# Attention's keys and values: one transfer over 128 partitions in place of two over 64

## The chip, the cores and the metric

The kernel runs on one core of a Trainium2 chip. The metric is device time in microseconds (us). The engines of the core are TensorE (PE in the profile: matrix products), VectorE (DVE), ScalarE (ACT), GpSimd (POOL) and SyncE (SP), which here issues every transfer. Sixteen DMA engines move the data between DRAM and the on-chip memory of 128 partitions.

## The reference

One pre-norm transformer block over 2,048 rows of 640 columns in float32: attention in a local, dilated window, then a gated feed-forward network.

```python
def _A_ref(x, wqkv, wo):
    H = 32; Dh = D // H                  # D = 640, Dh = 20
    W, dil = 8, 2
    qkv = (x @ wqkv).reshape(B, S, 3, H, Dh).transpose(2, 0, 3, 1, 4)
    q, k, v = qkv[0], qkv[1], qkv[2]
    idx = pos[:, None] - off[None, :]    # off = arange(W) * dil
    mask = idx >= 0
    ...
    logits = jnp.einsum("bhsd,bhswd->bhsw", q, kg) * Dh ** -0.5
    attn = softmax(where(mask, logits, -1e9))
    o = jnp.einsum("bhsw,bhswd->bhsd", attn, vg)
    return o.transpose(0, 2, 1, 3).reshape(B, S, D) @ wo

h = x + _A_ref(layernorm(x), wqkv, wo)
h2 = h + (silu(layernorm(h) @ w_gate) * (layernorm(h) @ w_up)) @ w_down   # F = 1728
```

Each row looks at itself and at the seven rows 2, 4, ..., 14 before it. Rows of even and of odd number never meet in attention; they are called the two parities below.

## The kernel before, in words

The 2,048 rows are cut into four blocks (b = 0 to 3) of 512. In a block, partitions 0 to 63 hold the 256 rows of one parity and partitions 64 to 127 those of the other, four consecutive rows of a parity (j) in each partition. The 32 heads are cut into four groups (g) of eight heads, 160 columns each. So attention has 16 steps (b, g).

`qkv` (line 532) computes queries, keys and values of one (b, g) on TensorE (line 552, in three passes that make up for the reduced precision of the products). ScalarE moves the sums into a staging tile `st` (line 557), which has room for two (b, g). From there `put` (line 563) stores the keys into the DRAM tensor `ksc` and the values into `vsc`, in two transfers each, one for each parity; the queries go to `qsc` in one (line 572). `ksc` and `vsc` have the shape [group, parity, 1,031 rows, 160 columns]; the first seven rows of each plane are zeros, the halo before the first row, which `zero_halo` (line 275) writes once in one transfer over 8 partitions for each tensor.

`att_load` (line 582) loads a step: the queries in two transfers (line 588), then keys and values (line 593). A partition needs its own four rows and the seven before, 11 rows of 160 columns or 7,040 bytes in one run, and neighbouring partitions' runs overlap: start every 640 elements, length 1,760. Again there is one transfer for each parity. Keys and values share three slots of 1,760 columns in turn, so the keys of one step take the place of the values of the step before the last, and its values that of the keys of the step before.

VectorE then does all of attention but the exponential: the products of queries and keys and their sums (`att_qk`, lines 603 and 610, twice per step), the maximum and the sum of the softmax (lines 617 to 634), the products with the values (line 638) and the sums over the window (line 646, lines 652 to 676). SyncE stores the result in 8 small transfers per step (line 680) into `osc`, from which the output projection `wo` (line 749, products at line 801) takes it. The feed-forward network of blocks 0, 1 and 2 (products at lines 871, 882, 966, 988) is computed between the attention steps; weights come from `ffn_in` (line 847), and their low-order parts go to DRAM once (`lsc`, line 860) and come back from there (lines 853, 1052, 1068).

What runs when is set by a planner. Every piece of work is put on record with an engine, a cost, what it reads and writes and a priority (`P.add`). `Plan.order` (line 74) plays these through with its own costs (for transfers: the bytes, the number of pieces and a fixed landing time) and so gets a start time for each piece; the table `SHIFT` moves the start times of some pieces, named by their number; the pieces are then written out in the order of these times, which fixes the order on each engine and on SyncE's queue. SyncE issues in that order, and waits at a transfer whose data or room are not there yet.

Of the kernel before, what the change touches and what calls it, by code (L numbers as in the profile page):

```python
# [20 lines left out]
NB, NJ, NG, NC = 4, 4, 4, 5  # L21
GC = D // NG
SEQ = S // 2 + W - 1
# [12 lines left out]
PR = {'x': 0.5, 'yst': 8, 'yld': 2, 'wqd': 4, 'wqh': 0.5, 'wql': 4, 'qev': 1, 'kvs': 0.4, 'atl': 1.2, 'exp': 0.5, 'ost': 3, 'wod': 2, 'woh': 8, 'wol': 1.2, 'old': 1.5, 'fld': 4, 'lst': 6, 'wev': 1.5, 'fh': 2.2, 'fl': 8, 'ln1': 8, 't1': 1, 'wo0': 1.2, 'wo': 2.2, 'ln1t': 1.2, 'xb': 0.4, 'tr': 10, 't1t': 2.2, 'ln1d': 0.5, 'hst': 10, 'hld': 10, 'ht': 1, 'hc': 2, 'jd': 3, 'jp': 8, 'js': 4, 'jl': 0.4, 'ja': 0.5, 'jfld': 1.2, 'jfh': 4, 'jfl': 1, 'jhi': 4, 'jmu': 0.4, 'jlo': 0.9, 'jcm': 0.5, 'w3': 1, 'w3e': 8, 'w3o': 0.4, 'w3x': 8, 'w3l': 2.2, 'jy': 6}  # L36

SHIFT = {
# [8 lines left out]
}  # L47


# [107 lines left out]
def nb(chunks, size):  # L157
    return (chunks / 16 * 0.042 + chunks * size / 435e3) * RATE


def act(n):
    return 0.155 + 0.00087 * n


def program(tc, x_in, wqkv_in, wo_in, ffn_in, ffl_in, const_in, out):
    nc = tc.nc
    V, A, T, Q, G = nc.vector, nc.scalar, nc.tensor, nc.sync, nc.gpsimd
    P = Plan()
# [4 lines left out]
    with tc.tile_pool(name="sb", bufs=1) as sb, tc.tile_pool(  # L173
        name="ps", bufs=1, space=PSUM
    ) as psp, tc.tile_pool(name="dr", bufs=1, space=DRAM) as dr, tc.manual_schedule():
        fa = sb.tile([128, FA_N], F32, name="fa")
# [30 lines left out]
        def stage_t():  # L207
            if "st" not in late:
                late["st"] = sb.tile([128, 3840], F32, name="st", tag="ab")
            return late["st"]  # L210
# [41 lines left out]
        def f(o, n):  # L252
            return fa[:, o : o + n]

        def rf(o, n):
            return ("fa", o, o + n)

        def r_(o, n):
            return ra[:, o : o + n]

        def rr(o, n):
            return ("ra", o, o + n)

        def pb(i):
            return (f"b{i}", 0, 1)
# [14 lines left out]
        for nm, t in (("K", ksc), ("V", vsc)):  # L280
            P.add(
                "SP", 0.07, lambda t=t: zero_halo(t), r=[rf(PROD, 1120)],
                w=[(f"{nm}{g}{a}", 0, 7) for g in range(NG) for a in range(2)], prio=6, nbytes=36e3,
# [180 lines left out]
        def wq(g, half, k):  # L464
            return 4800 * g + 2400 * half + 480 * k

        def xt(b):
            t = sha_t if b % 2 == 0 else (lambda: shb)
            nm = "sha" if b % 2 == 0 else "shb"
            return t, nm  # L470
# [61 lines left out]
        def qkv(b, g):  # L532
            t, nm = xt(b)
            so = 1920 * (qn[0] // NJ % 2)
            passes = ((0, 0), (1, 0), (0, 1))
            whole = [(p, c) for p in range(3) for c in range(NC)]
            if b == g == 0:
                whole = [x for c in range(NC + 1) for x in ([(0, c)] if c < NC else []) + ([(1, c - 1), (2, c - 1)] if c else [])]
            first_mm, last_mm = whole[0], whole[-1]
            for j in range(NJ):  # L540
                bk = qn[0] % 5
                qn[0] += 1
                moved = (b, g, j) == (NB - 1, NG - 1, NJ - 1)
                if moved:
                    P.add("ACT", act(640), lambda j=j: A.copy(r_(XH, 640), t()[:, 640 * j : 640 * j + 640].bitcast(F32)), r=[(nm, 640 * j, 640 * j + 640)], w=[rr(XH, 640)], prio=3)

                def mm(ps, j=j, bk=bk, moved=moved):
                    for p, c in ps:
                        a, w = passes[p]
                        o = 2560 * a + 640 * j + 128 * c  # L550
                        l = r_(XH + 128 * c, 128) if moved and a == 0 else t()[:, o : o + 128]
                        T.matmul(banks[bk][:, 0:480], l, r_(wq(g, w, c), 480), start=(p, c) == first_mm, stop=(p, c) == last_mm)  # L552
                for ps in [[x] for x in whole] if b == g == 0 else [whole]:
                    P.add("PE", 0.218 * len(ps), lambda ps=ps, mm=mm: mm(ps),
                          r=[x for p, c in ps for x in (rr(XH, 640) if moved and passes[p][0] == 0 else (nm, 2560 * passes[p][0] + 640 * j + 128 * c, 2560 * passes[p][0] + 640 * j + 128 * c + 128), rr(wq(g, passes[p][1], c), 480))],
                          w=[pb(bk)], prio=10)
                P.add("ACT", act(480) + 0.06, lambda bk=bk, j=j: A.activation(  # L557
                    stage_t()[:, so : so + 1920].rearrange("p (t j c) -> p t j c", t=3, j=NJ)[:, :, j, :],
                    banks[bk][:, 0:480].rearrange("p (t c) -> p t c", t=3), AF.Identity, scale=f(RS1 + 4 * b + j, 1)),
                    r=[pb(bk), rf(RS1 + 4 * b + j, 1)], w=[("ab", so + 480 * j, so + 480 * j + 480)], prio=PR["qev"])  # L560

            def put(par, dst, o):
                Q.dma_start(
                    dst[g, par, 7 + 256 * b : 7 + 256 * b + 256, :].rearrange("(r j) c -> r (j c)", j=NJ),
                    stage_t()[64 * par : 64 * par + 64, o : o + 640],
                )
            for nmd, dst, o in (("K", ksc, so + 640), ("V", vsc, so + 1280)):
                for par in range(2):
                    P.add("SP", 0.65, lambda par=par, dst=dst, o=o: put(par, dst, o), r=[("ab", so, so + 1920)],
                          w=[(f"{nmd}{g}{par}", 1000 + 256 * b, 1256 + 256 * b)], prio=PR["kvs"], nbytes=nb(64, 2560))  # L570
                if nmd == "K":
                    P.add("SP", 0.65, lambda: Q.dma_start(qsc[b, g].rearrange("p j c -> p (j c)"), stage_t()[:, so : so + 640]),
                          r=[("ab", so, so + 1920)], w=[(f"Q{b}{g}", 0, 4)], prio=PR["kvs"], nbytes=nb(128, 2560))
# [8 lines left out]
        def att_load(b, g):  # L582
            n = an[0]
            an[0] += 1
            ko, vo = KV + 1760 * (2 * n % 3), KV + 1760 * ((2 * n + 1) % 3)
            qo, lo, mo = QT, LG + 256 * (n % 2), MX + 64 * (n % 2)
            for h in range(2):
                P.add("SP", 0.45, lambda h=h: Q.dma_start(f(qo + 320 * h, 320), qsc[b, g, :, 2 * h : 2 * h + 2, :].rearrange("p j c -> p (j c)")), r=[(f"Q{b}{g}", 0, 4)], w=[rf(qo + 320 * h, 320)], prio=PR["atl"], nbytes=nb(128, 1280))
            for nmd, dst, o in (("K", ksc, ko), ("V", vsc, vo)):
                for par in range(2):  # L590
                    def ld(dst=dst, o=o, par=par):
                        a = dst[g, par, 256 * b, :]
                        Q.dma_start(fa[64 * par : 64 * par + 64, o : o + 1760],
                                    bass.AP(tensor=a.tensor, offset=a.offset, ap=[[640, 64], [1, 1760]]))
                    lo_r = 0 if b == 0 else 1000 + 256 * (b - 1)
                    P.add("SP", 0.45, ld, r=[(f"{nmd}{g}{par}", lo_r, 1000 + 256 * (b + 1))], w=[(f"fakv{par}", o, o + 1760)], prio=PR["atl"], nbytes=nb(64, 7040))
            return b, g, n, ko, vo, qo, lo, mo

        two_keys = []
# [586 lines left out]
        def ln2_columns(b, prio):  # L1186
# [8 lines left out]
            for u in range(5):  # L1195
# [9 lines left out]
              r=[rf(IDENT, 128)], w=[rf(IDENT, 128)], prio=0)  # L1205
# [13 lines left out]
        for b, g in first + last:  # L1219
# [13 lines left out]
            qkv(b, g)  # L1233
        todo = [(b, g) for b in range(NB) for g in range(NG)]
        cur = att_load(*todo[0])
        att_qk(0, *cur)
        for n in range(len(todo)):
# [99 lines left out]
```

## Time and profile before

| | |
|---|---|
| median of 3 runs | 845.46 us (845.4 to 845.81) |
| the profiled execution | 846.43 us |
| its span, first to last instruction | 844.5 us |
| TensorE busy | 837.2 us, 99% |
| VectorE busy | 707.4 us, 84% |
| ScalarE busy | 404.5 us, 48% |
| moved by DMA | 191.13 MB, 226 GB/s |
| share of the 16 DMA engines, the kernel's own queue | 71.8% |

The page gives an engine's busy time, its share of the span and its instructions. A DMA share is the mean over the 16 DMA engines. In the list of DMA issues a line names destination and source, the number of transfers, the size of one, and the median time from issue to landing. A DMA view over a stretch gives the packets that started in it, their bytes, and on the line of the queue `q1` the same packets, MB and their time as a share of 16 engines' time in that stretch. A row of the table by stage gives the stretch, its length, the busy time of each engine (and its instructions), the clock granted to TensorE, the DMA share and GB/s. In a group of instructions the numbers behind the bar are the busy time in us and the mean of one in ns, then the idle time of the engine ahead of them.

### The profile page before, as it was taken

To read this page: it belongs to the slowest core of one execution; us is meant where nothing else is said; L and a number is where in the kernel's file an instruction comes from. 1 tells how busy PE (TensorE), PEld (TensorE's weight loads), DVE (VectorE), ACT (ScalarE), POOL (GpSimd) and SP (SyncE) were. 2 spreads that over 40 slices of the span, in tenths; PEclk is the share of its full clock that TensorE was granted. 3 is DMA by queue.
4 is the path that set the end of the run, shared out by engine and by line. 5 is a ranking of instruction groups with operands and counts; after the bars stand their busy time and mean duration, and the time that the engine had idled before them with its cause. 6 is when DMAs were issued, how large, how long until landed. Compare 5 with 4: busy or idle time off the path is not lost.

```text
span 844.5 us, 10852 instructions
## 1 busy us (share of the span) xinstructions
PE 837.2 (99%) x3961; PEld 711.2 (84%) x3961; DVE 707.4 (84%) x841; ACT 404.5 (48%) x674; POOL 24.5 (3%) x33
## 2 busy tenths in 40 slices
PE   9999999999999999999999999999999999999998
PEld 7888888889888888888888888888888887888887
DVE  8889999999998999999999999999434986555652
ACT  7662553245753434875423566555447543333331
POOL 0000000000000100010000010000000000000000
PEclk9999999999999999999999999999999999999999
DMA  8899598778588879678997987977854564454432
GB/s 316 259 296 262 148 263 255 194 225 225 194 254 288 268 238 326 176 210 272 298 251 281 299 278 194 267 265 245 286 195 137 188 227 151 153 170 144 154 116 86
DMA packets 91253, 191.13 MB, mean 226 GB/s; under 512 B 32560, under 2 KB 51888, under 8 KB 90560
## 3 DMA queue, kind: packets, MB, share of 16 engines
q1 hardware_dynamic: 91200, 190.44, 71.8%
q8 instruction: 31, 0.51, 0.2%
q14 instruction: 22, 0.18, 0.1%
HBM read 144.26 MB, written 46.14 MB: 225 GB/s over the span
## 4 chain that ended last, share of the span: by engine, by line
PE 87%; DVE 8%; DMA 2%; issue 2%; ACT 0%; SPq 0%; DVEq 0%
PE bank L552 25%; PE bank L882 19%; PE bank L966 17%; PE bank L871 15%; PE bank L801 7%; PE bank L988 2%; DVE fa L638 2%; DMA fa<-ksc 2%; DVE fa L610 1%; DVE fa L603 1%; DVE fa L646 1%; PE bank L445 1%; DVE acts L917 1%; DVE ra L791 0%; DMA fa<-in_wqkv_dram 0%
## 5 line engine op out<-in xcount | busy, mean ns | idle before, releaser
L871 PE MATMUL bank<-shb,ra 128*128 128x512 f32 x810 | 189.9, 390 | 0.0
L871 PEld LDWEIGHTS bank<-shb,ra 128*128 128x128 f32 x810 | 151.6, 188 | 31.1
L882 PE MATMUL bank<-ra,acts 128*128 128x512 f32 (+1 forms) x662 | 163.0, 389 | 0.0
L882 PEld LDWEIGHTS bank<-ra,acts 128*128 128x128 f32 x662 | 122.5, 188 | 24.5
L552 PE MATMUL bank<-ra,sha 128*128 128x480 f32 x480 | 106.0, 380 | 0.4 <-ACT sha L515 0.4
L552 PE MATMUL bank<-ra,shb 128*128 128x480 f32 x470 | 102.8, 378 | 0.0
L552 PEld LDWEIGHTS bank<-ra,sha 128*128 128x128 f32 x480 | 89.5, 188 | 14.3 <-ACT sha L515 0.9
L552 PEld LDWEIGHTS bank<-ra,shb 128*128 128x128 f32 x470 | 88.0, 188 | 13.2
L603 DVE TENSOR_TENSOR fa<-fa 128x2560 f32<-128x2560 f32 x32 | 90.2, 2818 | 1.7 <-DMA ra<-lsc 0.9
L638 DVE TENSOR_TENSOR fa<-fa 128x2560 f32<-128x2560 f32 x32 | 90.3, 2822 | 0.8
L610 DVE TENSOR_REDUCE fa<-fa 128x128 f32<-128x2560 f32 x32 | 90.0, 2813 | 0.5
L966 PE MATMUL bank<-shb,ra 128*128 128x512 f32 x360 | 88.3, 391 | 0.6 <-DVE fa L1104 0.6
L557 ACT ACTIVATE st<-bank,fa 128x480 f32<-128x480 f32 x64 | 41.8, 660 | 97.5 <-PE bank L552 85.1
L966 PEld LDWEIGHTS bank<-shb,ra 128*128 128x128 f32 x360 | 67.0, 188 | 14.4 <-DVE fa L1104 1.0
L646 DVE TENSOR_TENSOR fa<-fa 128x1280 f32<-128x1280 f32 (+2 forms) x68 | 75.8, 1115 | 1.9 <-issue 0.4
L1104 DVE TENSOR_TENSOR fa<-bank,fa 128x512 f32<-128x512 f32 x60 | 41.2, 691 | 42.8 <-PE bank L966 41.8
L801 PE MATMUL bank<-ra 128*128 128x320 f32 x480 | 74.9, 309 | 1.0 <-DVE ra L791 1.0
L801 PEld LDWEIGHTS bank<-ra 128*128 128x128 f32 x480 | 72.4, 188 | 3.6 <-DVE ra L791 1.3
L966 PE MATMUL bank<-ra 128*128 128x512 f32 x288 | 68.4, 390 | 0.0
L966 PEld LDWEIGHTS bank<-ra 128*128 128x128 f32 x288 | 53.9, 188 | 11.7 <-ACT shb L1025 0.3
L848 ACT CAST ra<-fa 128x1280 fp32r<-128x1280 f32 (+1 forms) x38 | 45.9, 1207 | 32.8 <-PE bank L871 16.1
L916 ACT CAST acts<-fa 128x512 fp32r<-128x512 f32 x47 | 29.2, 620 | 60.1 <-DVE fa L906 33.7
(152 smaller groups left out, 842.3 us busy)
## 6 DMA issues: line engine op xcount, KB each, us to landing
fa<-in_ffn_dram SPq DMA_DIRECT2D x46, 960.0 KB, 7.1
ra<-lsc SPq DMA_DIRECT2D x45, 320.0 KB, 4.1
fa<-ksc SPq DMA_DIRECT2D x32, 440.0 KB, 5.9
fa<-vsc SPq DMA_DIRECT2D x32, 440.0 KB, 7.5
ra<-lsc SPq DMA_DIRECT2D x21, 640.0 KB, 5.4
lsc<-ra SPq DMA_DIRECT2D x13, 640.0 KB, 5.4
ksc<-st SPq DMA_DIRECT2D x32, 160.0 KB, 2.9
qsc<-st SPq DMA_DIRECT2D x16, 320.0 KB, 3.9
```

Of the source, the lines that this page charges most:

```text
L552: T.matmul(banks[bk][:, 0:480], l, r_(wq(g, w, c), 480), start=(p, c) == first_mm, stop=(p, c) == last_mm)
L557: P.add("ACT", act(480) + 0.06, lambda bk=bk, j=j: A.activation(stage_t()[:, so : so + 1920].rearrange("p (t j c) -> p t j c", t=3, j=NJ)[ ...
L603: P.add("DVE", dve(2560), lambda: V.tensor_tensor(f(PROD, 2560).rearrange("p (j w c) -> p j w c", j=2, w=W), window(ko, 2 * jp), f(qo + 32 ...
L610: P.add("DVE", dve(2560), lambda: V.tensor_reduce(f(lo + 128 * jp, 128), f(PROD, 2560).rearrange("p (n d) -> p n d", d=DH), axis=AX.X, op= ...
L638: V.tensor_tensor(f(PROD, 2560).rearrange("p (j w d) -> p j w d", j=2, d=DH), bass.AP(tensor=fa[:, vo : vo + 160].tensor, offset=fa[:, vo ...
L646: V.tensor_add(dst(v), v[:, :, 0:m, :], v[:, :, m : 2 * m, :])
L801: T.matmul(banks[bk][:, 0:320], l, r_(m, 320), start=p == 0 and c == 0, stop=p == 2 and c == NC - 1)
L848: P.add("ACT", act(n), lambda: A.copy(r_(gu, n), f(raw, n)), r=[rf(raw, n)], w=[rr(gu, n)], prio=PR["fh"])
L871: T.matmul(banks[bk], r_(gu + 1280 * w + wid * c + col, 128), x2(a, c), start=p == 0 and c == 0, stop=p == 2 and c == NC - 1)
L882: T.matmul(banks[bk][:, lo:hi], l, m, start=first and p == 0, stop=last and p == len(passes) - 1)
L966: T.matmul(banks[bk], r_(ws[w] + 256 * q, 128), x(a, c), start=start and p == n == q == 0, stop=stop and p == 2 and n == len(terms) - 1 an ...
L1104: dv(0, lambda: V.tensor_add(fb(h, dst), banks[bk], fb(h, src)), [pb(bk)] + fr(h, src), fr(h, dst))
```

## The change

The two stores of the keys become one over both parities, and so do the two stores of the values, the two loads of the keys and the two of the values. On the on-chip side the pattern is 128 partitions; on the DRAM side it gets a leading dimension of the two parities (2 planes, then 64 rows, then the run). What a transfer waits for and holds is the union of the two halves. The planner gets one piece with 128 runs in place of two with 64. Since pieces are numbered, the keys of `SHIFT` are renumbered, and six of its 73 entries are gone.

```diff
-            def put(par, dst, o):
+            def put(dst, o):
                 Q.dma_start(
-                    dst[g, par, 7 + 256 * b : 7 + 256 * b + 256, :].rearrange("(r j) c -> r (j c)", j=NJ),
-                    stage_t()[64 * par : 64 * par + 64, o : o + 640],
+                    dst[g, :, 7 + 256 * b : 7 + 256 * b + 256, :].rearrange("a (r j) c -> a r (j c)", j=NJ),
+                    stage_t()[:, o : o + 640],
                 )
             for nmd, dst, o in (("K", ksc, so + 640), ("V", vsc, so + 1280)):
-                for par in range(2):
-                    P.add("SP", 0.65, lambda par=par, dst=dst, o=o: put(par, dst, o), r=[("ab", so, so + 1920)],
-                          w=[(f"{nmd}{g}{par}", 1000 + 256 * b, 1256 + 256 * b)], prio=PR["kvs"], nbytes=nb(64, 2560))
+                P.add("SP", 0.65, lambda dst=dst, o=o: put(dst, o), r=[("ab", so, so + 1920)],
+                      w=[(f"{nmd}{g}{par}", 1000 + 256 * b, 1256 + 256 * b) for par in range(2)], prio=PR["kvs"], nbytes=nb(128, 2560))
...
             for nmd, dst, o in (("K", ksc, ko), ("V", vsc, vo)):
-                for par in range(2):
-                    def ld(dst=dst, o=o, par=par):
-                        a = dst[g, par, 256 * b, :]
-                        Q.dma_start(fa[64 * par : 64 * par + 64, o : o + 1760],
-                                    bass.AP(tensor=a.tensor, offset=a.offset, ap=[[640, 64], [1, 1760]]))
-                    lo_r = 0 if b == 0 else 1000 + 256 * (b - 1)
-                    P.add("SP", 0.45, ld, r=[(f"{nmd}{g}{par}", lo_r, 1000 + 256 * (b + 1))], w=[(f"fakv{par}", o, o + 1760)], prio=PR["atl"], nbytes=nb(64, 7040))
+                def ld(dst=dst, o=o):
+                    a = dst[g, 0, 256 * b, :]
+                    Q.dma_start(fa[:, o : o + 1760],
+                                bass.AP(tensor=a.tensor, offset=a.offset, ap=[[SEQ * GC, 2], [640, 64], [1, 1760]]))
+                lo_r = 0 if b == 0 else 1000 + 256 * (b - 1)
+                P.add("SP", 0.45, ld, r=[(f"{nmd}{g}{par}", lo_r, 1000 + 256 * (b + 1)) for par in range(2)], w=[(f"fakv{par}", o, o + 1760) for par in range(2)], prio=PR["atl"], nbytes=nb(128, 7040))
```

16 rows, old and new, of the table SHIFT are left out of this document.

## The prediction

> **What bounds the kernel now.** I read the page first, then the busy time by stage, the DMA issues, short windows of the DMA view, and the transfer queue in order of time.
>
> ```profile
> span 844.5 us, 10852 instructions
> PE 837.2 (99%) x3961; PEld 711.2 (84%) x3961; DVE 707.4 (84%) x841; ACT 404.5 (48%) x674; POOL 24.5 (3%) x33
> ...
> DMA packets 91253, 191.13 MB, mean 226 GB/s; under 512 B 32560, under 2 KB 51888, under 8 KB 90560
> ```
>
> ```profile
> core 0: us, PE busy (x) PEld busy (x) DVE busy (x) ACT busy (x) POOL busy (x), PEclk, DMA share, GB/s
> 0.00:22.70 22.70, 20.68 (x95) 17.03 (x96) 19.16 (x56) 16.22 (x37) 1.17 (x7) 1.00 0.89 319
> 22.70:240.00 217.30, 217.30 (x1069) 191.35 (x1068) 206.06 (x207) 105.40 (x203) 8.62 (x10) 1.00 0.79 234
> 240.00:530.00 290.00, 288.98 (x1365) 244.50 (x1364) 275.16 (x282) 148.61 (x222) 11.29 (x12) 1.00 0.84 258
> 530.00:844.50 314.50, 310.21 (x1437) 258.28 (x1435) 206.98 (x299) 134.26 (x217) 3.43 (x4) 1.00 0.55 185
> ```
>
> TensorE sets the time: it is idle for 844.5 - 837.2 = 7.3 us in all, not at all between 22.7 and 240 us, for 1.0 us between 240 and 530, and for 4.3 us after. So transfers that get quicker have almost nothing to win. But until 530 us the sixteen DMA engines are busy for 0.89, 0.79 and 0.84 of the time: the second resource stands close behind, and one that loses capacity there takes over.
>
> **The change, part by part.** These are the transfers it touches, the short ones, and the two that clear the halo, from the list of DMA issues (its first and last lines included; the 38 lines together count 588 transfers).
>
> ```profile
> fa<-in_ffn_dram SPq DMA_DIRECT2D x46, 960.0 KB, 7.1
> ...
> fa<-ksc SPq DMA_DIRECT2D x32, 440.0 KB, 5.9
> fa<-vsc SPq DMA_DIRECT2D x32, 440.0 KB, 7.5
> ...
> ksc<-st SPq DMA_DIRECT2D x32, 160.0 KB, 2.9
> ...
> vsc<-st SPq DMA_DIRECT2D x32, 160.0 KB, 3.9
> ...
> osc<-fa SPq DMA_DIRECT2D x112, 40.0 KB, 3.6
> ...
> zsc<-fa SPq DMA_DIRECT2D x8, 160.0 KB, 3.0
> ...
> ksc<-fa SPq DMA_DIRECT2D x1, 35.0 KB
> vsc<-fa SPq DMA_DIRECT2D x1, 35.0 KB
> fa<-in_const_dram SPq DMA_DIRECT2D x1, 16.0 KB, 4.2
> ```
>
> 64 loads of 440 KB become 32 of 880 KB, and 64 stores of 160 KB become 32 of 320 KB: 588 transfers become 524. Bytes, row lengths (7,040 and 2,560) and TensorE's order stay; VectorE and ScalarE each exchange two instructions with neighbours, which I cost at nothing because each stays within three places. What is new is the pattern on the DRAM side. Both halves were 64 rows. Now one pattern counts 2 parities outermost, then 64 rows, because the two parities lie a whole plane apart and cannot be folded into one run of 128 rows.
>
> How a transfer spreads over the engines decides everything. The trace has one kind with a small outermost count: the two halo transfers, 8 rows each. They alone have no landing time in the list above. And the short records count them: osc and zsc pieces are 256 B (64 floats), so 112 x 160 + 8 x 640 = 23,040, and the constants are 128 rows of 128 B; 32,560 - 23,168 = 9,392 short records are left. 588 transfers with one completion record from each of 16 engines would be 9,408. The missing 16 are what two transfers lack that close on 8 engines instead of 16. So the spread follows a count in the pattern and is not always 16.
>
> The trace does not say whether the count that matters is the outermost one or all rows, since both are 8 there. The bounds are therefore 16 engines (the 128 rows) and 2 (the outermost count, 2 on the DRAM side). I take 2: an outermost count that gave 8 engines is the one thing the halo shows, and a pattern with two levels gives the queue no single run of 128 to divide.
>
> [...]
>
> Now the price of two engines. These are four lines of the DMA view for 700.25 to 704.25 us (one weight load almost alone) and 837.3 to 841.8 (output stores of 2,560 B rows), then two for 493.6 to 498.1 (two halves of one 880 KB load).
>
> ```profile
> DMA packets 129, 0.87 MB, mean 217 GB/s; under 512 B 16, under 2 KB 16, under 8 KB 129
> ...
> q1 hardware_dynamic: 129, 0.87, 51.7%
> ```
>
> ```profile
> DMA packets 432, 0.98 MB, mean 218 GB/s; under 512 B 48, under 2 KB 48, under 8 KB 432
> ...
> q1 hardware_dynamic: 432, 0.98, 54.9%
> ```
>
> ```profile
> DMA packets 161, 0.90 MB, mean 200 GB/s; under 512 B 33, under 2 KB 33, under 8 KB 161
> ...
> q1 hardware_dynamic: 161, 0.90, 81.0%
> ```
>
> A load of long rows moves 0.87 MB / (0.517 x 4.0 us x 16) = 26.3 GB/s per busy engine, a store 0.98 / (0.549 x 4.5 x 16) = 24.8. The halves of K and V reach only 0.90 / (0.81 x 4.5 x 16) = 15.4, so today's 880 KB cost each of 16 engines 0.81 x 4.5 = 3.64 us.
>
> *Loads.* On two engines, each takes 450,560 B / 26.3 GB/s = 17.1 us. 32 loads: 548 us.
> *Stores.* 163,840 B / 24.8 GB/s = 6.6 us each; 32: 211 us.
> *Everything else on those two engines.* Until 530 us an engine is busy for 0.89 x 22.7 + 0.79 x 217.3 + 0.84 x 290 = 435 us. Of that 31 load pairs are 113 and 64 half stores, at 163,840 / 16 / 24.8 = 0.41, are 26; 296 us remain. With fourteen engines half empty there is less contention: the first stage's 319 / (0.89 x 16) = 22.4 GB/s against 26.3 would make it 250. I take 265, nearer the second.
>
> All other transfers use these two engines too and queue behind K and V, so nothing overtakes. That is 548 + 211 + 265 = 1,024 us of work in front of the last V load, for what took until 536.5 us.
>
> *Gaps.* The queue's order around attention, and VectorE's groups:
>
> ```profile
> 440.43 8.89 SPq L680 DMA_DIRECT2D osc<-fa  x8
> ...
> 529.47 1.09 SPq L593 DMA_DIRECT2D fa<-ksc  x2
> ...
> 536.49 0.45 SPq L593 DMA_DIRECT2D fa<-vsc  x1
> ```
>
> ```profile
> L603 DVE TENSOR_TENSOR fa<-fa 128x2560 f32<-128x2560 f32 x32 | 90.2, 2818 | 1.7 <-DMA ra<-lsc 0.9
> L638 DVE TENSOR_TENSOR fa<-fa 128x2560 f32<-128x2560 f32 x32 | 90.3, 2822 | 0.8
> L610 DVE TENSOR_REDUCE fa<-fa 128x128 f32<-128x2560 f32 x32 | 90.0, 2813 | 0.5
> L646 DVE TENSOR_TENSOR fa<-fa 128x1280 f32<-128x1280 f32 (+2 forms) x68 | 75.8, 1115 | 1.9 <-issue 0.4
> ```
>
> Three slots hold K and V. The next K is issued after the values of the step before and one half of the logits: 5.6 (L603, L610) + 2 x (2.8 + 2.2) (L638, two L646) + 5.6 = 21 us after K landed, and behind eight osc stores, here 8.9 us: some 30 us. Meanwhile the engines have V (17.1) and the step's share of other work (265 / 16 = 17): 34 us. That nearly covers it. If the cover is thin in every step it costs up to half of VectorE's 27 us, 216 in all; I take 5 us x 16 = 80. A merged load waits for the stores and the readers of both halves; these end together today too (one staging buffer, one VectorE instruction over all partitions), so the wait adds nothing, and what stands behind it on SP, queries and osc stores, waits for the backlog anyway. SP issues 64 transfers fewer, about 0.55 us each (1.09 for two above), hidden behind the same backlog.
>
> *The end.* After the last V load's place, with its landing (7.5 us, above), 844.5 - 536.5 - 7.5 = 300 us remain, and 310 of the last 314.5 are TensorE work that nothing shortens.
>
> Sum: 1,024 + 80 + 300 = 1,404 us of span. The profiled execution took 846.43 us (1.9 beside its span), 1.0 above the median 845.46, so the sum in the runs' terms is about **1,405 us**. The case's own range: 250 instead of 265, no gaps and a tail shortened by 40 us (TensorE may do ahead what now stands there) give 1,270; 296 and 216 give 1,575.
>
> [...]
>
> **The rivals.**
> *All sixteen engines, and faster.* If 128 rows are what is divided, a load costs 0.90 MB / (16 x 26.3) = 2.1 us instead of 3.64, as whole transfers would not share whatever holds the halves to 15.4 GB/s. That frees 32 x 1.5 = 48 us per engine, but only TensorE's 1.0 + 4.3 us of idle time can go: 843.5 us if a third does. It decides when more than 1.7 us (0.2%, about what these runs can tell from no change) of that idle time hangs on K and V. For it: the 15.4 against 26.3. Against: the halo's 8. [...]
> *Sixteen engines, no difference:* 845.5, TensorE stays the bound; a reordered wait could make 848.
> *Only the loads narrow* (the source's pattern decides): 548 + 26 + 265 + 80 + 300 = about 1,220. *Only the stores narrow* (the destination's decides): between 22.7 and 240 us the engine's 172 us become 172 - 58 - 25 + 34 + 30 x 6.6 = 321 against 217, so 950. [...]
>
> **How the numbers follow.** Two engines for both 0.80; loads only 0.05; stores only 0.04; sixteen engines 0.08 (faster 0.03, same 0.03, slower 0.02); something else, slower, 0.03. The forecast is the first. The range 1,200 to 1,600 holds nine tenths of it and the loads-only case, about 0.77. Faster 0.03, same 0.03, slower 0.94.
>
> **What would show it.** The long loads should land some 19 us or more after issue instead of 5.9 and 7.5, if they have a landing time at all; 64 stores and loads should leave 14 completion records each missing, 524 x 16 - 16 - 64 x 14 = 7,472 instead of 9,392. The DMA share should fall to about half of what it is until some 1,100 us while VectorE and TensorE wait for ksc and vsc loads; the last stage of about 300 us should look as before. Waits of the transfer queue for VectorE between loads would tell the gaps. Wrong it is if the loads land in 5 to 8 us and DMA share stays near 0.8.

## The result, and the profile after

The changed kernel takes 1,375.07 us (median of 5 runs, 1,373.94 to 1,376.09) against 845.54 us of the kernel before on the same chip: 1.6261 times as long, with a 95% interval of 1.6237 to 1.6284. 1,405 us was forecast, with a range of 1,200 to 1,600.

The page of the kernel after:

```profile
span 1373.4 us, 10768 instructions
...
PE 907.8 (66%) x3961; PEld 755.2 (55%) x3961; DVE 707.4 (52%) x841; ACT 401.8 (29%) x674; POOL 23.6 (2%) x33
...
DMA  7122322232221332273634373554235566464532
...
DMA packets 89332, 191.11 MB, mean 139 GB/s; under 512 B 30640, under 2 KB 49968, under 8 KB 88640
...
q1 hardware_dynamic: 89280, 190.43, 40.4%
```

TensorE is busy for 66% of the time instead of 99%. The DMA engines, which one would suspect next, seem even less busy than before: mostly one to three tenths in the first 550 us (16 of the 40 slices), 40.4% in the mean. But that is a mean over sixteen. The DMA view for 563 to 573 us, a stretch in which one load of 7,040 B rows was all that moved, shows what stands behind it:

```profile
DMA packets 76, 0.54 MB, mean 54 GB/s; under 512 B 0, under 2 KB 0, under 8 KB 76
...
q1 hardware_dynamic: 76, 0.54, 12.7%
```

12.7% of sixteen engines are two engines. The lone load runs at 54 GB/s, 0.54 MB / (0.127 x 10 us x 16) = 26.6 for each of the two. The short records say the same for all 64 merged transfers: 30,640 - 23,168 pieces of osc, zsc and constants = 7,472, just the number forecast (524 x 16 - 16 for the halo - 64 x 14). And the trace, which holds the start and the duration of every packet, has exactly two in flight on the kernel's queue for 614 of the 1,022 us between 22.7 and 1,044.6.

What waits, in the list of waits of the kernel after (engine and line, releaser, us in total, times, longest):

```profile
POOL fa L662 <- DVE fa L601: 1007.7, 12, 149.3
ACT st L557 <- DMA vsc<-st: 255.5, 10, 50.8
PEld bank L552 <- ACT st L557: 186.9, 10, 47.3
PE bank L552 <- ACT st L557: 182.6, 10, 46.9
DVE fa L601 <- DMA fa<-ksc: 139.0, 10, 32.6
ACT ra L846 <- DMA fa<-in_ffn_dram: 80.1, 8, 20.4
...
PE bank L869 <- DMA ra<-lsc: 76.5, 6, 28.5
```

Where the last stores and loads stand (issues of one line: shortest, median and longest duration in ns, first and last start in us). The first line is of the kernel before, the others of the kernel after:

```profile
L563 SPq DMA_DIRECT2D vsc<-st x32: 445/520/1043, 24.6 to 242.3; - x32
```

```profile
L563 SPq DMA_DIRECT2D vsc<-st x16: 493/650/14888, 24.1 to 576.0; - x16
L591 SPq DMA_DIRECT2D fa<-vsc x16: 500/1076/6357, 42.1 to 1044.6; - x16
```

GpSimd's wait in the first line says little: GpSimd is busy for 23.6 us in all. The longest wait that counts is one that the text ahead did not name: ScalarE cannot empty a bank (where TensorE leaves its sums) into the staging tile until the store of the values that used the tile has landed (255.5 us), and TensorE's products for queries, keys and values stand behind that (182.6). The last store leaves at 576.0 us instead of 242.3. Then VectorE waits for keys (139.0), and the feed-forward network, which has nothing to do with keys and values, waits for its weights (80.1 and 76.5). The likely reason is that the weights stand in the same queue and have a part of their rows on the same two engines: of the 128 rows of 7,680 B that were issued at 613.65 us, right behind the keys of 612.91, the trace has 112 started by 620.8 us and the other 16 from 633.2 on, when the keys' rows ran out (the last started at 633.6). And issuing one store alone held SyncE up for as long as 14.9 us, against 1.0 before. That wait was not tested by itself.

By stage (busy time and instructions of each engine, granted clock, DMA share, GB/s; cut at the last values load):

```profile
core 0: us, PE busy (x) PEld busy (x) DVE busy (x) ACT busy (x) POOL busy (x), PEclk, DMA share, GB/s
0.00:22.70 22.70, 20.97 (x94) 17.13 (x95) 18.95 (x56) 16.12 (x36) 1.17 (x7) 1.00 0.88 316
22.70:1044.60 1021.90, 583.21 (x2482) 485.91 (x2481) 492.10 (x496) 255.80 (x429) 20.70 (x24) 0.77 0.37 125
1044.60:1373.40 328.80, 303.58 (x1388) 252.19 (x1386) 196.35 (x291) 129.84 (x210) 1.71 (x2) 0.97 0.49 170
```

Of the 529 us lost, 508 lie before the last values load; behind it stand 328.8 us, against 308 before (844.5 - 536.5).

### The profile page after: what moved, and what is told of

The parts are those of the page before. It is cut to its first block, busy times and chain, and to the rows that moved or that the text cites. A ratio compares the mean times of both kernels' runs of the same rounds, so it can differ in the third digit from the quotient of the medians.

```text
span 1373.4 us, 10768 instructions
## 1 busy us (share of the span) xinstructions
PE 907.8 (66%) x3961; PEld 755.2 (55%) x3961; DVE 707.4 (52%) x841; ACT 401.8 (29%) x674; POOL 23.6 (2%) x33
## 2 busy tenths in 40 slices
DMA packets 89332, 191.11 MB, mean 139 GB/s; under 512 B 30640, under 2 KB 49968, under 8 KB 88640
## 3 DMA queue, kind: packets, MB, share of 16 engines
q1 hardware_dynamic: 89280, 190.43, 40.4%
## 5 line engine op out<-in xcount | busy, mean ns | idle before, releaser
L869 PE MATMUL bank<-shb,ra 128*128 128x512 f32 x810 | 207.6, 413 | 93.8 <-DMA ra<-lsc 76.5
L869 PEld LDWEIGHTS bank<-shb,ra 128*128 128x128 f32 x810 | 162.1, 202 | 132.0 <-DMA ra<-lsc 79.1
L552 PE MATMUL bank<-ra,shb 128*128 128x480 f32 x470 | 121.4, 422 | 117.5 <-ACT st L557 109.2
L601 DVE TENSOR_TENSOR fa<-fa 128x2560 f32<-128x2560 f32 x32 | 90.4, 2824 | 206.3 <-DMA fa<-ksc 139.0
L552 PEld LDWEIGHTS bank<-ra,shb 128*128 128x128 f32 x470 | 99.1, 213 | 138.3 <-ACT st L557 111.9
L880 PE MATMUL bank<-ra,acts 128*128 128x512 f32 (+1 forms) x662 | 171.0, 403 | 0.0
L552 PE MATMUL bank<-ra,sha 128*128 128x480 f32 x480 | 113.1, 396 | 73.7 <-ACT st L557 73.3
L880 PEld LDWEIGHTS bank<-ra,acts 128*128 128x128 f32 x662 | 128.8, 198 | 26.8
L799 PE MATMUL bank<-ra 128*128 128x320 f32 x480 | 84.8, 334 | 78.7 <-ACT ra L788 33.2
L799 PEld LDWEIGHTS bank<-ra 128*128 128x128 f32 x480 | 79.8, 207 | 83.9 <-ACT ra L788 34.9
L557 ACT ACTIVATE st<-bank,fa 128x480 f32<-128x480 f32 x64 | 39.9, 657 | 273.7 <-DMA vsc<-st 255.5
L964 PE MATMUL bank<-shb,ra 128*128 128x512 f32 x360 | 88.2, 391 | 0.6 <-DVE fa L1102 0.6
L846 ACT CAST ra<-fa 128x1280 fp32r<-128x1280 f32 (+1 forms) x38 | 45.8, 1205 | 118.0 <-DMA fa<-in_ffn_dram 80.1
L880 PE MATMUL bank<-acts,ra 128*128 128x512 f32 x164 | 50.0, 413 | 37.8 <-ACT acts L914 35.8
L964 PEld LDWEIGHTS bank<-shb,ra 128*128 128x128 f32 x360 | 67.0, 188 | 14.4 <-DVE fa L1102 1.0
L964 PEld LDWEIGHTS bank<-ra 128*128 128x128 f32 x288 | 53.9, 188 | 11.7 <-ACT shb L1023 0.4
```

The costliest lines, as they stand in the source:

```text
L601: P.add("DVE", dve(2560), lambda: V.tensor_tensor(f(PROD, 2560).rearrange("p (j w c) -> p j w c", j=2, w=W), window(ko, 2 * jp), f(qo + 32 ...
L799: T.matmul(banks[bk][:, 0:320], l, r_(m, 320), start=p == 0 and c == 0, stop=p == 2 and c == NC - 1)
L846: P.add("ACT", act(n), lambda: A.copy(r_(gu, n), f(raw, n)), r=[rf(raw, n)], w=[rr(gu, n)], prio=PR["fh"])
L869: T.matmul(banks[bk], r_(gu + 1280 * w + wid * c + col, 128), x2(a, c), start=p == 0 and c == 0, stop=p == 2 and c == NC - 1)
L880: T.matmul(banks[bk][:, lo:hi], l, m, start=first and p == 0, stop=last and p == len(passes) - 1)
L964: T.matmul(banks[bk], r_(ws[w] + 256 * q, 128), x(a, c), start=start and p == n == q == 0, stop=stop and p == 2 and n == len(terms) - 1 an ...
```

## The experiments

The theory: the outermost count of a transfer's pattern sets over how many engines it spreads, and the two engines that carry keys and values set the time. The rivals: the merged pieces, their waits and their order cost the time; or a transfer over two planes is slow in any form; or only one of the two directions is narrow. Where nothing else is said, the experiments change the kernel after, in the patterns alone, and keep its plan.

**Two halves in the new plan.** Each merged piece issues its two old transfers.

```diff
                 def ld(dst=dst, o=o):
-                    a = dst[g, 0, 256 * b, :]
-                    Q.dma_start(fa[:, o : o + 1760],
-                                bass.AP(..., ap=[[SEQ * GC, 2], [640, 64], [1, 1760]]))
+                    for par in range(2):
+                        a = dst[g, par, 256 * b, :]
+                        Q.dma_start(fa[64 * par : 64 * par + 64, o : o + 1760],
+                                    bass.AP(..., ap=[[640, 64], [1, 1760]]))
```

(and `put` in the same way)

> The changed kernel's plan, its order and its 32 merged pieces are kept, but each piece issues its two 64-row transfers again, with a pattern of 64 rows outermost. Theory 'two engines' (the pattern with the count of 2 outermost is all of the loss): 845 to 849 us, loads land in 6 to 8 us, 9,392 short completion and data records of the old kind return. Rival 'the plan' (merged pieces wait for both halves and the new order is what costs): well over 1,000 us, near 1,375.

Measured: 845.64 us, 1.0002 times the kernel before (0.9993 to 1.0011). Its page counts 32,560 short records again. So pieces, waits and order cost nothing by themselves; the loss comes with the pattern.

**Only the loads merged; only the stores merged.** The halves of the diff above for `put` alone, then for `ld` alone.

> Only the loads keep the merged pattern; the stores are two 64-row transfers again. Theory 'two engines, for loads and stores alike': loads 548 us on the two engines, stores 26, other work 265, gaps 80, tail 300: about 1,220 us, 155 us under the changed kernel. Rival 'only one direction is narrowed, by the destination's pattern': 845 to 850. Rival 'only by the source's': 1,375, as in the changed kernel.

> Only the stores keep the merged pattern; the loads are two 64-row transfers again. Theory 'two engines, for both alike': the first 240 us grow by about 104, 950 us. Rival 'only by the destination's pattern': 1,375. Rival 'only by the source's': 845 to 850. A store's 6.6 us on two engines should be seen in the wait of ScalarE for the staging tile.

Measured: 1,206.56 us with the loads merged, 966.39 with the stores merged (one timed run each). Both directions are narrowed, whichever side the pattern with two planes is on: source in the loads, destination in the stores. Both sums came within 17 us. With the stores merged, ScalarE's wait for the staging tile is 104.9 us, as was looked for. The excesses over 845.57, 361 and 121, add up to 482 of the 529 that both together cost.

**Rows outermost.** Still one transfer over 128 partitions and two planes, but the partitions alternate between the parities (inputs, mask and output are dealt out to match), so that the pattern counts 64 rows first.

```diff
-                    dst[g, :, 7 + 256 * b : ...].rearrange("a (r j) c -> a r (j c)", j=NJ),
+                    dst[g, :, 7 + 256 * b : ...].rearrange("a (r j) c -> r a (j c)", j=NJ),
...
-                                bass.AP(..., ap=[[SEQ * GC, 2], [640, 64], [1, 1760]]))
+                                bass.AP(..., ap=[[640, 64], [SEQ * GC, 2], [1, 1760]]))
```

> One transfer over 128 partitions as in the changed kernel, but partitions alternate between the parities, so that the DRAM pattern counts 64 rows outermost and 2 parities inside. Theory 'the outermost count decides': sixteen engines, 842 to 848 us; a load of 880 KB costs each engine 2.1 us in place of 3.64, as long rows over all partitions run at 26 GB/s; TensorE's idle time stays near 7 us, so hardly a gain over before. Rival 'a pattern of two levels is narrow in any order, or a transfer over two planes is': near 1,375. Rival 'quick loads pay': under 840.

Measured: 845.73 us, 1.0002 times the kernel before (0.9993 to 1.001). Two dimensions changed places, and 529 us are gone. The page, and two lines of its DMA issues:

```profile
PE 837.5 (99%) x3961; PEld 711.5 (84%) x3961; DVE 706.6 (84%) x841; ACT 404.9 (48%) x674; POOL 23.6 (3%) x33
...
DMA packets 90228, 191.12 MB, mean 227 GB/s; under 512 B 31536, under 2 KB 50864, under 8 KB 89536
...
q1 hardware_dynamic: 90176, 190.44, 66.0%
...
fa<-ksc SPq DMA_DIRECT2D x16, 880.0 KB, 5.1
fa<-vsc SPq DMA_DIRECT2D x16, 880.0 KB, 6.3
```

8,368 completion records are 524 x 16 less the halo's 16: all sixteen engines. This is the transfer the change was made of, without its fault: 880 KB land in 5.1 and 6.3 us, where 440 KB took 5.9 and 7.5, and the engines are busy for 66.0% instead of 71.8%, some 50 us less for each. Yet the time is that of the kernel before, because TensorE is busy for 837.5 us as ever. The gain of a good merge is real, and hidden.

The loads themselves came out slower than expected. The DMA view for 193.5 to 197 us shows one, almost alone:

```profile
DMA packets 144, 0.91 MB, mean 260 GB/s; under 512 B 15, under 2 KB 15, under 8 KB 143
...
q1 hardware_dynamic: 143, 0.90, 78.8%
```

It takes 0.788 x 3.5 = 2.8 us of each engine, 0.90 MB / (2.8 us x 16) = 20 GB/s, not the 2.1 us at 26 GB/s of the expectation.

**Counts of 2, 4 and 8.** Transfers over 64 partitions again, but the rows of a half are dealt to its partitions in another order (inputs, mask and output to match), so that the pattern has two levels that don't fold. The cut starts from the two halves of the first run; n is the count, and the stores get the same two levels.

```diff
                     for par in range(2):
                         a = dst[g, par, 256 * b, :]
                         Q.dma_start(fa[64 * par : 64 * par + 64, o : o + 1760],
-                                    bass.AP(..., ap=[[640, 64], [1, 1760]]))
+                                    bass.AP(..., ap=[[640, n], [n * 640, 64 // n], [1, 1760]]))
```

> Transfers over 64 partitions as before, but the rows of a half are dealt to its partitions in another order, so that the pattern counts 2 outermost and 32 inside. Theory 'the outermost count decides, not the size or the two planes': two engines again, the same 759 us of keys and values on each, about 1,375 us (1,340 to 1,420). Rival 'all rows count, 64 rows are sixteen engines': 845 to 850. Rival 'the two planes are what is narrow': 845 to 850.

> The same with a count of 4 outermost and 16 inside. Theory: four engines, keys and values 380 us on each, with 265 of other work 645 us before the last load of values, plus a tail of 300 and gaps of 0 to 80: 945 to 1,025 us. Rival 'only counts under a threshold matter': 845.

> The same with a count of 8 outermost and 8 inside. Theory: eight engines, keys and values 190 us on each, with 265 to 296 of other work 455 to 486 us, less than the 536 that the place of the last load takes in the kernel before: no longer the bound, 845 to 850 us. A half's load on eight engines at 26.3 GB/s takes 2.1 us and on sixteen at 15.4 GB/s 1.8 us, so its landing should stay near 6 us.

Measured: 1,408.08 us for 2, 1,071.21 for 4 (one timed run each), 906.64 for 8 (1.0702 times the kernel before, 1.0668 to 1.0736). Halves with a count of 2 make the kernel as slow as the merged transfers do, so neither size nor the second plane is to blame. The records follow the count. In the order 2, 4, 8, from the three pages:

```profile
DMA packets 89461, 191.12 MB, mean 136 GB/s; under 512 B 30768, under 2 KB 50096, under 8 KB 88768
```

```profile
DMA packets 89717, 191.12 MB, mean 179 GB/s; under 512 B 31024, under 2 KB 50352, under 8 KB 89024
```

```profile
DMA packets 90229, 191.13 MB, mean 211 GB/s; under 512 B 31536, under 2 KB 50864, under 8 KB 89536
```

Less 23,168 these are 7,600, 7,856 and 8,368: 9,392 short by 128 transfers times 14, 12 and 8. The time falls in the order forecast, but for 4 and 8 it was above the forecast, and 8 was not free.

For 4, the DMA view for 275 to 279 us (loads nearly alone) and for 0 to 758 us (the last values load starts at 758.2):

```profile
DMA packets 65, 0.43 MB, mean 107 GB/s; under 512 B 4, under 2 KB 4, under 8 KB 65
...
q1 hardware_dynamic: 65, 0.43, 25.6%
```

```profile
DMA packets 67671, 136.15 MB, mean 180 GB/s; under 512 B 26099, under 2 KB 42643, under 8 KB 66995
...
q1 hardware_dynamic: 67635, 135.69, 57.4%
```

25.6% are four engines, at 26 GB/s each. The 758 us hold 0.574 x 758 x 16 = 6,962 us of engine time. At that rate 31 loads (27.9 MB) and all stores (10.5 MB at 24.8) are 1,066 + 423 = 1,489 of it, 372 on each of the four; the rest, if it spreads evenly, is 342 on each of the sixteen, where I had 265. By this estimate 714 of 758 us are work. It is a low one, because the loads ran slower beside other transfers: their rows took 1,406 us by the trace, not 1,066. With that the same sum gives 457 + 321 = 778, a little more than there is. Either way the four engines are the bound, under slower loads and more other work than assumed.

For 8, the view for 274 to 277.5 us (one half of a load) and 0 to 598 us (the last values load starts at 598.0):

```profile
DMA packets 86, 0.46 MB, mean 132 GB/s; under 512 B 19, under 2 KB 19, under 8 KB 86
...
q1 hardware_dynamic: 86, 0.46, 51.0%
```

```profile
DMA packets 67918, 135.53 MB, mean 227 GB/s; under 512 B 26566, under 2 KB 43014, under 8 KB 67242
...
q1 hardware_dynamic: 67882, 135.08, 76.2%
```

51.0% are eight engines, but each moves 0.46 / (0.51 x 3.5 x 16) = 16 GB/s, not the 26.3 that I had put in. So 31 loads and all stores cost 27.9 MB / 16 + 423 = 2,167 us of engine time, 271 on each of the eight. The 598 us hold 0.762 x 598 x 16 = 7,291; the rest, if it spreads evenly, is 320 on each engine. 271 + 320 = 591 of 598: by this estimate these eight are hardly ever idle, and in the trace there are 13 us between 22.7 and 598 without a packet in flight. The expectations failed by the rate and by the other work, not by the rule of the count.

**Every other partition.** Why are half transfers on eight and sixteen engines slow per engine, 15 to 16 GB/s? Starting from the kernel with rows outermost, two transfers again, each for one parity and over every other partition of all 128.

```diff
-                    stage_t()[:, o : o + 640],
+                    stage_t()[par : 128 : 2, o : o + 640],
...
-                Q.dma_start(fa[:, o : o + 1760], ...)
+                    Q.dma_start(fa[par : 128 : 2, o : o + 1760], ...)
```

> The partitions alternate between the parities as in the run with rows outermost, but each store and load is again two transfers of 64 rows, now over every other partition of all 128 in place of 64 neighbours. Question: what holds halves to 15 GB/s per engine. Theory 'neighbouring partitions share a way into the memory, half of them means half of the ways': pieces now run at 20 to 26 GB/s, the DMA share of the kernel's own queue falls from 71.9% to about 66%. Rival 'a row or transfer count effect: 64 rows on sixteen engines are slow wherever they land': 15 GB/s and 72% stay. The time says little, 845 to 848 us in both, since TensorE bounds it.

Measured: 986.49 us, 1.1669 times the kernel before (1.1638 to 1.1701), which nobody expected, and half loads that land faster than in any other run that shows their landing. The DMA view for 202.5 to 206 us (both halves of a load), two lines of the DMA issues, and a line of what VectorE's window sums (L646) waited for:

```profile
DMA packets 160, 0.90 MB, mean 257 GB/s; under 512 B 32, under 2 KB 32, under 8 KB 160
...
q1 hardware_dynamic: 160, 0.90, 72.9%
```

```profile
fa<-ksc SPq DMA_DIRECT2D x32, 440.0 KB, 4.4
fa<-vsc SPq DMA_DIRECT2D x32, 440.0 KB, 4.2
```

```profile
  DMA fa<-ksc: 61.2, 12
```

An engine moves 0.90 / (0.729 x 3.5 x 16) = 22 GB/s, against 15.4 for the same 64 rows to neighbouring partitions and 20 for the whole transfer with rows outermost. The shares of the pages agree: 57.3% of 982.7 us are 563 us for each engine, where whole transfers took 557 (66.0% of 843.5) and neighbouring halves 607 (71.9% of 844.0). So it is the neighbourhood that slows the halves, and not their number of rows. The time answers another question. L646 reads products, not keys, and yet waits for keys loads. It looks as if a strided slice of the large tile `fa` is ordered against parts of it that it does not touch; this was read from the list of waits and not tried by itself. So the time of this run can't be set against the others.

## Why the prediction was right

**Two engines.** Right, in both directions. It rested on the halo's 16 missing records and left open whether the outermost count or all rows decide; the run with rows outermost and the run with a count of 2 in one plane settle that it is the outermost count, as far as it was tried: at 2, 4, 8 and 64 a transfer left 14, 12, 8 and no completion records fewer than 16. The prediction's other reason, that a pattern with two levels leaves no single run to divide, did not hold: rows outermost has two levels, 8,368 records and 845.73 us.

**Loads and stores, 548 + 211 us.** The rate of the loads held: 26.6 GB/s in the lone load above, against 26.3; beside other transfers it fell, to 24.8 in the mean of the trace's 4,096 rows of 7,040 B. No store was seen alone, so the 211 us rest on the rate of other stores. The loads have no landing time in the new profile, as was left possible.

**Other work on the two engines, 265 us: too small by 40.** The view of the kernel after for 0 to 1,046 us:

```profile
DMA packets 67142, 135.65 MB, mean 130 GB/s; under 512 B 25706, under 2 KB 42199, under 8 KB 66468
...
q1 hardware_dynamic: 67108, 135.21, 37.9%
```

That is 0.379 x 1,046 x 16 = 6,343 us of engine time. Thirty and a half loads (27.5 MB at 26.3 GB/s, 1,045; the rows of the last keys load ran from 1,034.0 to 1,054.9) and all stores (423) are 1,468 of it, 734 on each of the two; the rest, if it spreads evenly, is 305 on each engine. My 265 came from the belief that transfers get quicker when fourteen engines are half empty. They did not. The same sum for the kernel before, up to the issue of its last values load, is 82.4% of 536.5 us, or 442, less 113 and 26: 303. (The 296 of the prediction went to 530 us and took off 31 loads, where 30 were done; with 30 it is 300.)

**Gaps, 80 us: too large by some 70.** 734 + 305 = 1,039 of 1,046, so by this sum the two engines were idle for 7 us. As a difference of two large estimates that is uncertain by some 30 us (with the 1,111 us that the rows of the loads took by the trace, in place of 1,045, it comes out below nothing), but the trace says much the same: no packet is in flight for 11 of the 1,022 us from 22.7 to 1,044.6. The sign that the prediction named, SyncE waiting for VectorE before a load, is there and small:

```profile
SPq L591 <- DVE fa L636: 22.8, 9, 5.5
```

The cover that I called nearly complete, 34 us against 30, was about complete; 305 / 16 = 19 us of other work in a step made it thicker.

**The end, 300 us.** It was 327.4, counted from 1,046. I had put all 32 loads in front of that point; half of the last keys load and the last values load were still to be moved when it came. So 25 us too much in front (759 against 734) and 27 too little behind: they nearly cancel. With 40 too little and 73 too much above, that is 31 too much in all, which is what lies between the sum of 1,404 and the span of 1,373.4. The forecast owes part of its accuracy to misses of opposite sign. One reading of the prediction was incomplete: in the kernel before the last values load is issued in two halves, at 536.5 and at 564.6 us, and the prediction took the first for the whole. The merged load stands in the first one's place in the queue, so the sum did not suffer. (The upper end of the prediction's own range, 1,575, adds up to 1,572.)

**The clock.** The forecast has no term for it. The granted clock fell to 0.77 in the mean between 22.7 and 1,044.6 us, where TensorE was busy for 583.21 of 1,021.9 us, and TensorE's busy time grew from 837.2 to 907.8 us. Two stretches of the table by stage, the first with TensorE busy, the second with TensorE idle:

```profile
100.00:106.00 6.00, 6.00 (x29) 5.22 (x28) 0.00 (x0) 0.00 (x0) 0.00 (x0) 1.00 0.14 57
112.00:118.00 6.00, 0.00 (x0) 0.00 (x0) 0.00 (x0) 0.00 (x0) 0.00 (x0) 0.50 0.13 53
```

The granted clock is 1.00 in the first and 0.50 in the second. The two engines set the time and were hardly ever idle (no packet in flight for 11 of 1,022 us), and TensorE's extra 71 us lay beside them. They all fall before the last values load (604.2 us busy up to it, against 533.5 before); behind it TensorE is busy for 303.6 us, against 303.7.

**The rivals.** Loads only, 1,220, and stores only, 950, were named as other rules of the chip; as edits they came to 1,206.56 and 966.39. The one on the other side, sixteen engines and faster, had the direction right and its gain wrong: 845.73 against 843.5. The run with rows outermost freed some 50 us per engine, against my 48, but that nearness is luck: the load seen alone took 2.8 us of each engine, not 2.1, and by the trace all rows of the loads went from 119 to 82 us per engine. The other 13 us came from other transfers. TensorE's idle time went from 7.3 to 6.0 us in the profiles, and the runs show no gain from that.

## What to carry to other kernels

Put the large count outermost in a transfer's pattern, here 64 rows (845.73 us) and not 2 planes (1,375.07); merging two transfers under a leading dimension of 2 cost far more here than the second issue, 529 us against 64 issues of some 0.5 us. Look for it in the profile as a DMA share that is low while everything waits for DMA: the lone load with a share of 12.7% ran on two engines. And ask first whether the transfers are on the path: here a good merge freed some 50 us on every DMA engine and gained nothing.

## What the runs showed of the hardware

How fast a DMA engine moves the 7,040 B rows of keys and values depends on how they are spread. Mean time of one row over all 4,096 of a run, by its trace:

| transfers | engines | ns for a row | GB/s per engine |
|---|---|---|---|
| halves, 64 neighbouring partitions | 16 | 477 | 14.8 |
| the same, count of 8 | 8 | 463 | 15.2 |
| the same, count of 4 | 4 | 353 | 20.0 |
| the same, count of 2 | 2 | 299 | 23.5 |
| halves, every other partition | 16 | 333 | 21.1 |
| whole, rows outermost | 16 | 319 | 22.1 |
| whole, planes outermost | 2 | 284 | 24.8 |

In the kernel before, the neighbouring halves took 464 ns, 15.2 GB/s. That half as many engines don't lift the rate of neighbouring halves (477 and 463 ns) was unexpected. These are means: with counts of 4 and 8, the rows of a single half took between some 270 and 600 or 700 ns in the mean, and the lone load with a count of 4 above ran at 26 GB/s. What holds them back, and why it holds eight engines as it does sixteen while four are held less, was not tried and stays open.
